# An attention and MLP kernel: eight lead tiles whose scores read the keys in place, and a first block of full-width chunks

## The chip, the core and the metric

The kernel runs on one core of a Trainium2 chip. The metric is device time in microseconds, the median of the timed runs. TensorE (PE) multiplies, VectorE (DVE), ScalarE (ACT) and GpSimd (POOL) work elementwise, SyncE (SP) issues all loads and stores here. A core's engines run side by side, each through its own list in order, and wait for each other by semaphores.

## The reference

Two batches of 768 positions, 8 heads of 64. Each query sees the keys less than 16 positions away and, for every block of 32 keys, one summary key (the maximum over the block) with the mean of its values. The result, 1536 tokens of 512, goes through two layers of MLP (the last two pieces below, 2048 wide inside).

```python
k_sum = k.reshape(B, H, nb, block, D).max(axis=3)
v_sum = v.reshape(B, H, nb, block, D).mean(axis=3)
scores_l = scale * np.matmul(q, k.transpose(0, 1, 3, 2))
...
scores_s = scale * np.einsum('bhsd,bhnd->bhsn', q, k_sum)
scores_s = scores_s + np.log(block)
...
a = np.exp(scores_all)
a = a / (np.sum(a, axis=-1, keepdims=True) + 1e-09)
v_all = np.concatenate([v, v_sum], axis=2)
return np.matmul(a, v_all).astype(np.float32)
...
h = np.maximum(x @ w_in, 0.0)
return (h * h @ w_out).astype(np.float32)
...
h = x @ w_in
g = h * (1.0 / (1.0 + np.exp(-h)))
return (g @ w_out).astype(np.float32)
```

## The kernel before

**Attention** goes by 24 tiles of 64 queries, tiles 0 to 11 for the first batch. A tile's 8 heads are four pairs, two heads on the 128 partitions. `scores` (pss) makes 96 window columns and 24 summary columns at once: two matmuls of 64x120 for each pair. `minima` takes mask and row minimum on VectorE, `exps` the exponentials and their sums z on ScalarE, `inverse` and `norm` scale by 1/z, `transposes` (psa) turns the tile on TensorE, ScalarE copies it (a), `products` (av) multiplies by the values, and `x_high` and `x_low` (xh, xl) split the result into a high and a low half in xt.

**The MLP** goes by three blocks of 512 tokens (eight tiles each) and 16 chunks of the weights. A gemm is 12 matmuls: four parts by three products of high and low halves. gemm1 of chunk s makes h, ScalarE makes relu, square and the high half of g, VectorE the low half (gl), and gemm2 adds to four accumulators (acc). The first layer's weights come as 64-bit floats and are decoded on the fly, chunk by chunk (wi for gemm1, wo for gemm2): ScalarE scales (sc), VectorE shifts, joins sign and low bits (sh, st1, st2), ScalarE writes the high half (hi), VectorE the low one (lo). That is four VectorE steps for each of 32 half chunks, all of them in the first block. Later blocks reuse the split weights.

**The lead.** Tiles 0 to 3 come first. Their key windows are cut by ScalarE (kwl, 16 copies) from the four key tiles of the whole batch, which VectorE also reduces to the 24 maxima (ksum) and copies behind each window (kwsum). Tiles 4 to 7 load their windows and queries as all later tiles do, by two buffers. With four tiles done, the first two chunks begin with 256 columns (TRAIL = 2, HALF = 256); from chunk 2 on 512 columns are taken; and the other 256 columns of chunks 0 and 1 come after chunk 15 as chunks 16 and 17. In the meantime tiles 8 to 15 are worked between the gemms, and the second batch's keys and values are loaded in 16 pieces (kv) and reduced (kvr), each load waiting for the reduction two before it.

**What sets the order.** `first_order` is a list planner: each operation has an engine, a duration, a due time and what it waits for; it takes the operation that can start first and, among those, the one due first. The result is the program order of VectorE, ScalarE, TensorE and SP for the whole first block. From block 1 on a scheduler sets it.

## Time and profile before

| | us |
|---|---|
| median of 3 runs | 626.02 (625.27 to 626.58) |
| profiled execution | 624.39 |
| its span | 622.6 |
| TensorE busy in the span | 603.9 (97%) |
| VectorE busy | 341.4 (55%) |
| ScalarE busy | 302.3 (49%) |

The profile gives each engine's busy time, who released it from a wait, and the clock that TensorE was granted (1.00 is 2.4 GHz, 0.50 is 1.2 GHz). A matmul's start to the next one's start is its price in a row of matmuls; the end in the record holds a tail that overlaps the next. The share of busy time over the whole span says little here, since the first 160 us are another stage than the rest; the tables by stage do. The span leaves out 1.8 us around it.

### The profile page before, as it was taken

How to read it: one execution, taken by the hardware profiler on the slowest of the kernel's cores; microseconds unless marked ns; L12 is line 12 of the kernel's file. 1: busy time of each engine (PE TensorE's matmuls, PEld its weight loads, DVE VectorE, ACT ScalarE, POOL GpSimd, SP SyncE). 2: the span in 40 equal slices, each digit the busy share in tenths (PEclk: the TensorE clock that was granted, in tenths of full speed). 3: DMA queues.
4: the chain of work that ended last, by engine and by line, in shares of the span. 5: the costliest groups of instructions: out<-in, count | busy, mean ns of one | idle time of the engine just before them, and what ended most of it. 6: DMA issues, size and time to landing. Idle time of an engine off the chain costs nothing.

```text
span 622.6 us, 8963 instructions
## 1 busy us (share of the span) xinstructions
PE 603.9 (97%) x3252; PEld 488.1 (78%) x3252; DVE 341.4 (55%) x795; ACT 302.3 (49%) x687; POOL 55.0 (9%) x64
## 2 busy tenths in 40 slices
PE   7789997999999999999999999999999999999997
PEld 5477785777888877888888888888888888888886
DVE  5898998993356444465555686665322222322222
ACT  5876976887535454365454564443222221322221
POOL 0120000000453333100000000000000000000000
PEclk9987999999999999999999999999999999999999
DMA  8987888762455555547653424425400123400301
GB/s 304 313 285 229 263 274 287 229 209 85 141 191 176 185 170 201 172 141 237 200 178 129 136 100 163 178 100 202 152 19 1 67 102 102 135 1 0 102 34 69
DMA packets 37292, 97.51 MB, mean 157 GB/s; under 512 B 4096, under 2 KB 11904, under 8 KB 37248
## 3 DMA queue, kind: packets, MB, share of 16 engines
q1 hardware_dynamic: 37248, 96.93, 47.2%
q8 instruction: 26, 0.43, 0.3%
q14 instruction: 18, 0.15, 0.1%
HBM read 75.94 MB, written 20.97 MB: 156 GB/s over the span
## 4 chain that ended last, share of the span: by engine, by line
PE 78%; DVE 12%; DMA 7%; ACT 1%; SPq 1%; issue 1%; DVEq 0%; ACTq 0%
PE acc L222 37%; PE h L222 37%; DMA t_kv<-in_kT_dram 2%; DMA raw_wi<-in_w_in_dram 2%; PE av L222 2%; DMA raw_wo<-in_w_out_dram 1%; PE pss L222 1%; DMA t_kv<-in_vT_dram 1%; DVE c_wo L282 1%; DVE wi L230 1%; DVE raw_wo L278 1%; DVE raw_wi L278 1%; DVE c_wi L282 1%; DVE wo L230 1%; DVE T L402 1%; DVE g L230 1%
## 5 line engine op out<-in xcount | busy, mean ns | idle before, releaser
L222 PE MATMUL h<-xt,wi 128*128 128x512 f32 (+1 forms) x600 | 146.5, 392 | 3.2 <-DVE wi L230 2.0
L222 PE MATMUL acc<-g,wo 128*128 128x512 f32 (+1 forms) x600 | 141.7, 386 | 0.0
L222 PE MATMUL h<-xt,wj 128*128 128x512 f32 x576 | 139.0, 391 | 0.0
L222 PEld LDWEIGHTS h<-xt,wi 128*128 128x128 f32 x600 | 109.1, 192 | 27.1 <-DVE wi L230 2.8
L222 PEld LDWEIGHTS acc<-g,wo 128*128 128x128 f32 x600 | 110.1, 191 | 22.5 <-issue 0.6
L222 PEld LDWEIGHTS h<-xt,wj 128*128 128x128 f32 x576 | 108.1, 188 | 23.6 <-DVE r L230 0.2
L230 DVE TENSOR_TENSOR g<-r,g 128x512 fp32r<-128x512 f32 (+1 forms) x98 | 80.4, 820 | 79.9 <-ACT g L226 40.7
L230 DVE TENSOR_TENSOR r<-h,r 128x512 f32<-128x512 f32 x48 | 33.2, 691 | 114.2 <-ACT r L529 113.7
L529 ACT ACTIVATE r<-h 128x512 f32<-128x512 f32 x48 | 28.7, 598 | 117.4 <-PE h L222 117.4
L226 ACT ACTIVATE g<-r 128x512 fp32r<-128x512 f32 (+1 forms) x82 | 50.9, 621 | 35.5 <-DVE r L230 34.6
L222 PE MATMUL acc<-wq,g 128*128 128x512 f32 x240 | 57.3, 389 | 0.0
L222 PE MATMUL acc<-wo,g 128*128 128x512 f32 x216 | 53.6, 397 | 0.0
L222 PEld LDWEIGHTS acc<-wq,g 128*128 128x128 f32 x240 | 45.1, 188 | 9.3
L222 PEld LDWEIGHTS acc<-wo,g 128*128 128x128 f32 x216 | 40.7, 188 | 9.7
L411 ACT ACTIVATE T<-T,m 128x120 f32<-128x120 f32 x96 | 36.7, 384 | 20.4 <-DVE m L402 20.3
L222 PE MATMUL acc<-wp,g 128*128 128x512 f32 x120 | 28.8, 389 | 0.0
L227 POOL COPY qd<-qr 128x256 f32<-128x256 f32 x20 | 16.6, 831 | 135.0 <-PE pss L222 97.0
L226 ACT ACTIVATE wo<-c_wo 128x512 fp32r<-128x512 f32 x38 | 23.6, 622 | 7.3 <-DVE c_wo L282 7.2
L521 ACT ACTIVATE r<-h 128x512 f32<-128x512 f32 x16 | 9.6, 598 | 34.7 <-PE h L222 34.7
L222 PEld LDWEIGHTS acc<-wp,g 128*128 128x128 f32 x120 | 22.5, 188 | 4.7
L230 DVE TENSOR_TENSOR wj<-c_wj,wj 128x512 fp32r<-128x512 f32 x16 | 11.1, 692 | 23.7 <-ACT wj L226 23.7
L402 DVE CUSTOM_DVE_ANT_0 T<-pss,cst_sb 128x120 f32<-128x120 f32 x96 | 21.1, 274 | 5.0 <-PE pss L222 4.9
(77 smaller groups left out, 576.9 us busy)
## 6 DMA issues: line engine op xcount, KB each, us to landing
raw_wo<-in_w_out_dram SPq DMA_DIRECT2D x22, 512.0 KB, 4.2
wq<-split SPq DMA_DIRECT2D x20, 512.0 KB, 3.3
raw_wi<-in_w_in_dram SPq DMA_DIRECT2D x16, 512.0 KB, 5.2
split<-wo SPq DMA_DIRECT2D x16, 512.0 KB, 3.4
raw_wj<-in_w_in_dram SPq DMA_DIRECT2D x16, 512.0 KB, 3.7
...
```

The costliest lines, as they stand in the source:

```text
L222: pe.matmul(o, l, r, **kw)
L226: return act.activation(out=o, in_=i, func=AF.Copy, scale=scale)
L227: return eng.tensor_copy(out=o, in_=i)
L230: return eng.tensor_tensor(out=o, in0=a, in1=b, op=op)
L278: vec.scalar_tensor_tensor(out=low, in0=high, scalar=SIGN, in1=low, op0=ALU.bitwise_and, op1=ALU.bitwise_or)
L282: vec.scalar_tensor_tensor(out=c, in0=c, scalar=3, in1=raws.pop(name)[:, :, 0], op0=ALU.logical_shift_left, op1=ALU.bitwise_or)
L402: vec.tensor_tensor_reduce(out=T[:, c], in0=ps[:, c], in1=cst_sb[:, kind * NK:kind * NK + NK], scale=-0.125, scalar=3.0e38, op0=ALU.add, o ...
L411: act.activation(out=T[:, c], in_=T[:, c], func=AF.Exp, bias=m[:, c:c + 1], scale=-1.0, accum_out=z[:, c:c + 1])
L521: act.activation(out=r, in_=h, func=AF.Relu)
L529: act.activation(out=r, in_=h, func=AF.Sigmoid)
```

## The change

NLEAD goes from 4 to 8, and TRAIL and HALF go. Every tile of the first block is now in the lead. Their scores read the keys where they lie: for a tile g and a pair hp the matmul takes 96 columns of the batch's key tile (with 16 zero columns ahead of it) at g x 64, and another one the 24 maxima. So there are no window copies, no copies of maxima behind them and no loads of windows and queries for tiles 4 to 7. The lead's scores (psl), minima (ttl) and exponentials (exl) are planned by pairs instead of whole tiles; queries and values come in two groups of four tiles; the key tiles are loaded with the first queries and the masks between them. The value means are copied to the lead's tiles by two ScalarE copies of 2048 columns (four of 512 before), and to the two buffers of later tiles by ScalarE instead of GpSimd (vfm). Scores and products of the lead use the four accumulator banks. All 16 chunks of the first block take 512 columns. The due times move, and the planner now takes, among the operations of one engine that can start within 0.1 us, the one due first.

```diff
-HALF = 256
-TRAIL = 2
...
-NLEAD = 4
+NLEAD = 8
+NGRP = 4
...
-        return .5 * g if g < NLEAD else 14 + 3 * (g - NLEAD) if g < 2 * NLEAD else 48 + 11 * (g - 2 * NLEAD)
+        return .25 * g if g < NLEAD else 46 + 11 * (g - NLEAD)
...
-    for hp in range(NHP):
-        load("kt", hp, 393, -100 + hp)
-    load("q", 0, 524, -90)
-    load("cst", 0, 250, -89)
-    for c in range(3):
-        load("vr", c, 524, -88 + c)
-    load("vl", 0, 786, -80)
+        return 30 + 7 * s
+
+
+    for i, (name, arg, kb) in enumerate([("kt", 0, 393), ("q", 0, 524), ("kt", 1, 393), ("cst", 0, 250), ("kt", 2, 393),
+                                         ("kt", 3, 393), ("q", 1, 524), ("vr", 0, 524), ("vr", 1, 524), ("vr", 2, 524),
+                                         ("vl", 0, 786), ("vl", 1, 786)]):
+        load(name, arg, kb, -100 + i)
     for hp in range(NHP):
         op("vec", "ksum", hp, 1.0, -50 + hp, [("kt", hp, 0)])
-        op("act", "kwl", hp, .85, -50 + hp, [("kt", hp, 0)])
-    op("vec", "kwsum", 0, .57, -40, [("ksum", hp, 0) for hp in range(NHP)])
...
-        op("pe", "vs", c, .92, 1.2 + .5 * c, [("vr", c // 2, 0)] + [("vs", c - 1, 0)] * (c > 0))
-    op("act", "vmean", 0, 2.2, 3, [("vs", 5, M)])
+        op("pe", "vs", c, .92, 1.7 + .1 * c, [("vr", c // 2, 0)])
+    for i in range(NLEAD // NGRP):
+        op("act", "vmean", i, 1.9, -5, [("vs", c, M) for c in range(6)] + [("vl", i, 0)] * 0)
+    for i in range(NVF):
+        op("act", "vfm", i, .6, tile_due(NLEAD) - 10 + i, [("vmean", 0, 0)])
...
-            op("pe", "pss", g, 1.22, due, [("kwl", hp, A) for hp in range(NHP)] + [("kwsum", 0, A), ("q", 0, 0)])
-            op("vec", "ttr", g, .84, due, [("pss", g, M), ("cst", 0, 0)])
+            for hp in range(NHP):
+                op("pe", "psl", (g, hp), .38, due, [("kt", hp, 0), ("ksum", hp, A), ("q", g // NGRP, 0)] +
+                   [("psl", (g, hp - 1), 0)] * (hp > 0), bank=None if hp else ("acc", "ttl", (g, NHP - 1)))
+                op("vec", "ttl", (g, hp), .21, due, [("psl", (g, hp), M), ("cst", 0, 0)])
+                op("act", "exl", (g, hp), .385, due, [("ttl", (g, hp), A)])
+            exp = [("exl", (g, hp), A) for hp in range(NHP)]
...
-        if g < 2 * NLEAD:
-            op("vec", "nt", g, .78, due, [("zr", g, 0)])
+            op("pe", "pss", g, 1.1, due, [("kwc", g, A), ("side", g, A)] + [("gemm1", 1, 0)] * (g == NLEAD), bank=("att", "ttr", g))
+            op("vec", "ttr", g, .84, due, [("pss", g, M), ("psa", g - 2, M)])
+            op("act", "exp", g, 1.54, due, [("ttr", g, -.45)])
+            exp = [("exp", g, A)]
+        op("vec", "ze", g, .09, due, exp)
+        op("vec", "rc", g, .1, due, [("ze", g, .1)])
+        if g < NLEAD:
...
-    for s in range(NF + TRAIL):
-        due = chunk_due(s) if s < NF else chunk_due(NF - 1) + 6 + 3 * (s - NF)
-        wide = TRAIL <= s < NF
-        p, a, v = (2.72, .57, .61) if wide else (1.44, .34, .36)
-        x = [("xl", g, A) for g in range(NLEAD if s < TRAIL else 2 * NLEAD)]
-        op("pe", "gemm1", s, p, due, x + [("lo", ("wi", s % NF), A)] + [("relu", s - 2, A)] * (s >= 2))
-        op("act", "relu", s, a, due, [("gemm1", s, M)] + [("gl", s - 2, A)] * (s >= 2))
-        op("act", "sq", s, a, due, [("relu", s, 0)])
-        op("act", "gh", s, a, due, [("sq", s, 0)] + [("gemm2", s - 3, M)] * (s >= 3))
-        op("vec", "gl", s, v, due, [("gh", s, A)])
-        op("pe", "gemm2", s, p, due + 5 * LAG, [("gl", s, A), ("lo", ("wo", s % NF), A)] + [("gemm2", s - 1, 0)] * (s > 0))
+    for s in range(NF):
+        due = chunk_due(s)
+        op("pe", "gemm1", s, 2.72, due, [("xl", g, A) for g in range(NLEAD)] + [("lo", ("wi", s), A)] +
+           [("relu", s - 2, A)] * (s >= 2))
+        op("act", "relu", s, .57, due, [("gemm1", s, M)] + [("gl", s - 2, A)] * (s >= 2))
+        op("act", "sq", s, .57, due, [("relu", s, 0)])
+        op("act", "gh", s, .57, due, [("sq", s, 0)] + [("gemm2", s - 3, M)] * (s >= 3))
+        op("vec", "gl", s, .61, due, [("gh", s, A)])
+        op("pe", "gemm2", s, 2.72, due + 5 * LAG, [("gl", s, A), ("lo", ("wo", s), A)] + [("gemm2", s - 1, 0)] * (s > 0))
...
+        t, _, _, o = min((p for p in picks if p[3]["eng"] == o["eng"] and p[0] <= t + .1), key=lambda p: p[1:3])
...
+            T = wo_p.tile([P, NHP, NK], F32, tag="wo", name=f"T{g}") if g < NWO else p2.tile([P, NHP, NK], F32, tag="T", name=f"T{g}")
+            st[g] = dict(v=vlead[:, g], T=T, a=wi_p.tile([P, 512], F32, tag="wi", name=f"a{g}"))
+            small(g)
+        for hp in range(NHP):
+
+            kts[hp] = first_p.tile([P, WIN + S], F32, tag=f"kt{hp}", name=f"t_ksum0_{hp}")
+            pool.memset(kts[hp][:, 0:WIN], 0.0)
...
-        def kwl(hp):
-            for g in range(NLEAD):
-                lo = WIN if g == 0 else 0
-                copy(act, kws[g][:, hp, lo:NWIN], kts[hp][:, g * QT - WIN + lo:g * QT - WIN + NWIN])
-
-        def kwsum(_):
-            for g in range(NLEAD):
-                k_sums(g)
+
+        def psl(ghp):
+            g, hp = ghp
+            if hp == 0:
+                st[g]["ps"] = ps_acc.tile([P, NHP, NK], F32, tag="acc", name=f"pss{g}")
+            q = qrlead[g // NGRP][:, g % NGRP].rearrange("p (q c) -> p c q", c=NHP)
+            for keys, to in ((kts[hp][:, g * QT:g * QT + NWIN], slice(0, NWIN)), (ksum[0][:, hp], slice(NWIN, NK))):
+                for e in range(2):
+                    pr = slice(64 * e, 64 * e + 64)
+                    mm(st[g]["ps"][pr, hp, to], q[pr, hp], keys[pr], start=True, stop=True)
...
-        def vmean(_):
-            for g in range(NLEAD):
-                copy(act, vlead[NWIN:NK, g].rearrange("p h d -> p (h d)"), psv[NWIN:NK])
-            for v in vf:
-                copy(pool, v[NWIN:NK], vlead[NWIN:NK, 0])
+        def vmean(i):
+            means = psv[NWIN:NK]
+            copy(act, vlead[NWIN:NK, i * NGRP:i * NGRP + NGRP].rearrange("p g h d -> p g (h d)"),
+                 bass.AP(means.tensor, means.offset, [means.ap[0], [0, NGRP], means.ap[1]]))
+
+        def vfm(i):
+            copy(act, vf[i][NWIN:NK], vlead[NWIN:NK, 0])
...
-        def cols(s):
-            return slice(HALF if s >= NF else 0, HALF if s < TRAIL else 2 * HALF)
-
         def gemm1_(s):
             h = hs[s] = ps_h.tile([P, 512], F32, tag="h", name=f"h0_{s}")
-            cc = cols(s)
-            gemm1(wi1[s % NF], x, cc.start, cc.stop - cc.start, h[:, cc])
+            gemm1(wi1[s], x, 0, 512, h)
...
-            gemm2(accs, ws["wo", s % NF], gs.pop(s), cc.start, cc.stop - cc.start, s == 0, s == NF + TRAIL - 1, check=False)
+            gemm2(accs, ws["wo", s], gs.pop(s), 0, 512, s == 0, s == NF - 1)
```

On VectorE, at the start: the four key tiles' maxima (ksum), then the copies behind the windows, then minima tile by tile (an ISA row is one minimum of a pair with its accumulator). Before:

```order
L604 TENSOR_REDUCE ksum0_162<-t_ksum0_0_144 128x24
L604 TENSOR_REDUCE ksum0_162<-t_ksum0_1_146 128x24
L604 TENSOR_REDUCE ksum0_162<-t_ksum0_2_148 128x24
L604 TENSOR_REDUCE ksum0_162<-t_ksum0_3_150 128x24
L227 COPY kw0_139<-ksum0_162 128x4x24
L227 COPY kw1_140<-ksum0_162 128x4x24
L227 COPY kw2_141<-ksum0_162 128x4x24
L227 COPY kw3_142<-ksum0_162 128x4x24
L402 ISA T0_226,m0_227<-pss0_208,cst_sb_98 128x120
L402 ISA m0_227 128x1
```

and now:

```order
L615 TENSOR_REDUCE ksum0_201<-t_ksum0_0_180 128x24
L615 TENSOR_REDUCE ksum0_201<-t_ksum0_1_182 128x24
L397 ISA T0_140,m0_142<-pss0_211,cst_sb_98 128x120
L397 ISA m0_142 128x1
L397 ISA T1_145,m1_147<-pss1_218,cst_sb_98 128x120
L397 ISA m1_147 128x1
L397 ISA T2_150,m2_152<-pss2_225,cst_sb_98 128x120
L397 ISA m2_152 128x1
L397 ISA T3_155,m3_157<-pss3_230,cst_sb_98 128x120
L397 ISA m3_157 128x1
L397 ISA T0_140,m0_142<-pss0_211,cst_sb_98 128x120
L397 ISA m0_142 128x1
```

The copies are gone, and the minima of the first pairs stand ahead of the maxima of the last two key tiles.

On TensorE, between the lead's transposes (psa) and the first accumulations: products av of tile g, scores pss, h0_s is gemm1 of chunk s. Before:

```order
L222 MATMUL av0_404<-a0_298,vlead_104 64x64 x8
L222 MATMUL av1_429<-a1_324,vlead_104 64x64 x8
L222 MATMUL av2_449<-a2_342,vlead_104 64x64 x8
L222 MATMUL av3_467<-a3_352,vlead_104 64x64 x8
L432 MATMUL psa4_486<-cst_sb_98,T4_380 120x128 x4
L432 MATMUL psa5_495<-cst_sb_98,T5_415 120x128 x4
L222 MATMUL h0_0_503<-xt0_85,wi0_358 128x256 x12
L222 MATMUL av4_524<-a4_500,vfr0_105 64x64 x8
L222 MATMUL av5_537<-a5_516,vfr1_106 64x64 x8
L222 MATMUL h0_1_554<-xt0_85,wi1_520 128x256 x12
L222 MATMUL pss6_581<-kw6_386,qd0_101 64x120 x8
L222 MATMUL pss7_596<-kw7_413,qd1_102 64x120 x8
```

and now:

```order
L229 MATMUL av0_556<-a0_141,vlead_105 64x64 x8
L229 MATMUL av1_569<-a1_146,vlead_105 64x64 x8
L229 MATMUL av2_580<-a2_151,vlead_105 64x64 x8
L229 MATMUL av3_591<-a3_156,vlead_105 64x64 x8
L229 MATMUL av4_606<-a4_161,vlead_105 64x64 x8
L229 MATMUL av5_619<-a5_166,vlead_105 64x64 x8
L229 MATMUL av6_633<-a6_171,vlead_105 64x64 x8
L229 MATMUL av7_647<-a7_176,vlead_105 64x64 x8
L229 MATMUL pss9_662<-kw9_241,qd1_102 64x120 x8
L229 MATMUL h0_0_681<-xt0_85,wi0_511 128x512 x12
L229 MATMUL h0_1_709<-xt0_85,wi1_656 128x512 x12
L229 MATMUL h0_2_742<-xt0_85,wi2_722 128x512 x12
```

Eight products in a row and one tile's scores now stand ahead of the first gemm, and the first three gemms are of 512 columns.

On TensorE, at the end of the first block (av15 is the last tile's product; acc0_0 to acc0_3 are the accumulators). Before, from chunk 15 on:

```order
L432 MATMUL psa15_1863<-cst_sb_98,T15_1812 120x128 x4
L222 MATMUL h0_16_1868<-xt0_85,wi0_358 128x256 x12
L222 MATMUL av15_1883<-a15_1881,vfr1_106 64x64 x8
L222 MATMUL h0_17_1895<-xt0_85,wi1_520 128x256 x12
L222 MATMUL acc0_0_619<-g0_15_1860,wo15_1762 128x512 x3
```

and now:

```order
L229 MATMUL acc0_3_772<-g0_13_1781,wo13_1677 128x512 x3
L229 MATMUL av15_1859<-a15_1850,vfr1_107 64x64 x8
L229 MATMUL h0_15_1868<-xt0_85,wi15_1824 128x512 x12
L229 MATMUL acc0_0_769<-g0_14_1856,wo14_1740 128x512
L229 MATMUL pss16_2029<-kw16_1956,qd0_101 64x120 x4
L229 MATMUL acc0_0_769<-g0_14_1856,wo14_1740 128x512 x2
L229 MATMUL acc0_1_770<-g0_14_1856,wo14_1740 128x512 x3
```

The half-width h0_16 and h0_17 are gone, and the scores of tile 16, of block 1's attention, stand among the accumulations of chunk 14.

## Rows read from the trace of the kernel before

**Rows 1.** Stages: start:end, length, each engine's busy us (instructions), clock, DMA share, GB/s.

```profile
3.80:48.63 44.83, 36.00 (x352) 26.73 (x350) 37.99 (x158) 34.34 (x119) 5.80 (x8) 0.90 0.94 306
...
61.50:145.70 84.20, 79.39 (x522) 61.44 (x520) 77.57 (x204) 67.95 (x174) 6.60 (x8) 1.00 0.77 244
...
161.00:622.60 461.60, 458.01 (x2218) 374.74 (x2216) 210.89 (x400) 181.00 (x353) 39.27 (x36) 1.00 0.37 125
```

**Rows 2.** Timeline of TensorE: start, us, line, op, out<-in, shape, count; the first block's accumulations.

```profile
48.63 2.93 PE L222 MATMUL acc<-g,wo 128*128 128x256 f32 x12
...
160.03 2.91 PE L222 MATMUL acc<-g,wo 128*128 128x256 f32 x23
```

**Rows 3.** Waits of TensorE, 61.5 to 146 us: who waited for whom, us, times, longest.

```profile
PE h L222 <- DVE wi L230: 2.0, 2, 1.1
PE h L222 <- ACT wi L226: 1.2, 1, 1.2
```

**Rows 4.** Timeline of TensorE, 60 to 69 us.

```profile
60.55 1.04 PE L222 MATMUL pss<-kw,qd 64*64 64x120 f32 x16
61.52 3.03 PE L222 MATMUL h<-xt,wi 128*128 128x512 f32 x12
...
67.12 0.60 PE L432 MATMUL psa<-cst_sb,T 128*120 128x128 f32 x4
67.64 1.04 PE L222 MATMUL pss<-kw,qd 64*64 64x120 f32 x16
```

**Rows 5.** Timeline of TensorE in the lead.

```profile
1.46 6.60 PE L222 MATMUL idle_out<-idle_in 128*128 128x512 f32 x20 [1.46 <-DVE idle_in L576]
10.26 3.14 PE L222 MATMUL pss<-kw,qrlead 64*64 64x120 f32 x48 [2.20 <-DVE kw L227]
13.33 1.04 PE L222 MATMUL psv<-vrows,share 128*24 128x512 f32 x2
...
25.82 0.68 PE L222 MATMUL av<-a,vlead 120*64 120x64 f32 x16
```

**Rows 6.** Weight loads for scores: count, ns min/median/max; strided queries, then packed ones.

```profile
L222 PEld LDWEIGHTS pss<-kw,qrlead x64: 190/213/214, 10.2 to 15.1; 64*64 64x64 f32 x64
...
L222 PEld LDWEIGHTS pss<-kw,qd x16: 130/134/134, 60.6 to 61.2; 64*64 64x64 f32 x16
```

**Rows 7.** Timeline of VectorE: one tile's z to the next minimum, and four minima on.

```profile
13.50 0.17 DVE L417 TENSOR_SCALAR z<-z 128x4 f32<-128x4 f32 x1
...
14.69 0.28 DVE L402 CUSTOM_DVE_ANT_0 T<-pss,cst_sb 128x120 f32<-128x120 f32 x1
...
15.50 0.17 DVE L417 TENSOR_SCALAR z<-z 128x4 f32<-128x4 f32 x1
```

**Rows 8.** Timeline of VectorE: two xl; the first steps of two successive decodes.

```profile
29.04 0.75 DVE L230 TENSOR_TENSOR xt<-av,xt 128x256 fp32r<-128x256 f32 x2
...
50.71 0.42 DVE L274 TENSOR_SCALAR raw_wo<-raw_wo 128x512 int32<-128x512 int32 x1
...
53.11 0.42 DVE L274 TENSOR_SCALAR raw_wi<-raw_wi 128x512 int32<-128x512 int32 x1
```

**Rows 9.** Timelines of VectorE and ScalarE: last maxima, copies of maxima, value means.

```profile
7.74 2.01 DVE L604 TENSOR_REDUCE ksum<-t_ksum 128x24 f32<-128x768 f32 x2 [1.79 <-DMA t_ksum<-in_kT_dram]
9.79 0.57 DVE L227 COPY kw<-ksum 128x96 f32<-128x96 f32 x4
...
22.63 2.04 ACT L226 ACTIVATE vlead<-psv 24x512 f32<-24x512 f32 x4 [0.28 <-PE psv L222]
```

**Rows 10.** Stretches of 2 us, columns as in rows 1.

```profile
28.00:30.00 2.00, 0.66 (x16) 0.52 (x12) 1.97 (x8) 1.98 (x7) 0.00 (x0) 0.78 1.05 396
...
34.00:36.00 2.00, 2.00 (x11) 2.00 (x11) 1.93 (x4) 1.10 (x2) 0.86 (x1) 0.52 0.49 191
36.00:38.00 2.00, 2.00 (x41) 1.80 (x40) 2.00 (x5) 1.73 (x7) 0.00 (x0) 1.00 0.67 223
```

**Rows 11.** Chain that ended last, from 80 us: start, us, what.

```profile
80.39 5.88 DMA t_kv<-in_kT_dram
```

More of the change, by code (lines that the diff above doesn't have):

```diff
@@ L389, in scores, with minimum @@
         st[g]["ps"] = ps
-    def minima(g):
+    def minimum(g, c):
         d = st[g]
@@ L500, in att_steps @@
                 exps(i)
+                guard(i)
                 inverse(i)
@@ L551, in gemm1, with gemm2 @@
             mm(h, w[:, 1, ws], xh, start=False, stop=(k == NKC - 1))
-    def gemm2(acc, w, g, c0, n, first, last, check=True):
+    def gemm2(acc, w, g, c0, n, first, last):
         for k in range(NKC):
@@ L557, in gemm2 @@
             gh, gl = g[:, 0, c0:c0 + n], g[:, 1, c0:c0 + n]
[L558 to L561 removed]
+            mm(o, w[:, 0, ws], gh, start=first, stop=False)
+            mm(o, w[:, 0, ws], gl, start=False, stop=False)
+            mm(o, w[:, 1, ws], gh, start=False, stop=last)
     def finish1(x, acc):
```

151 lines of the change are left out of this document (70 added, 81 removed).

## The prediction

> **What bounds the kernel now.** I read the table by stages first: from 161.0 us to the end TensorE is busy 458.0 of 461.6 us [rows 1], so nothing that the first block does can hide behind the rest, and whatever moves the end of the first block moves the end of the kernel by as much. The change touches only what runs ahead of that point. Second, the first block itself. From 61.5 to 145.7 us TensorE is busy 79.4 of 84.2 us and VectorE 77.6 [rows 1]: two engines are full at once, TensorE a little more so. TensorE's 4.8 us of waits there are mostly for decoded weights [rows 3]. Third, the lead: from 3.8 to 48.63 us TensorE runs 36.0 of 44.8 us, but in it stand only three half-width gemms (a gemm is 12 matmuls, of one weight chunk with the block's columns). The first block's last matmuls, 24 of 256 columns for the two trailing halves, end at 162.9 us with 1.8 us of block 1's work among them [rows 2], so the block's own list ends at about 161.1.
>
> So I keep a ledger: block 1 can start when TensorE has done its list. With A the start of the first full gemm in the changed kernel, the end of the block is A plus the list's work plus waits plus what a low clock costs.
>
> **The list.** One full gemm: in 61.5 to 145.7 us stand 22 gemms, seven tiles' attention and one small transposition group. A tile costs 0.97 us for scores (60.55 to 61.52), 0.52 for transposes (67.12 to 67.64) [rows 4] and 0.61 to 0.68 for the products [rows 5], 2.1 us together. (79.4 - 7 x 2.1 - 0.4) / 22 = 2.92 us. After A the changed kernel has 16 chunks x 2 gemms and tiles 8 to 15: 32 x 2.92 + 8 x 2.1 + 0.4 = 110.6 us. The same sum for the kernel before, from 48.63 us: one half gemm at half clock 2.7, 28 full ones 81.8, four trailing halves 5.9 (2.9 for the two that accumulate [rows 2], 3.0 for the two ahead of them), tiles 17.2, waits 4.8, makes 161.0, which is what the trace has. The trailing halves themselves are worth little: eight halves at 1.5 against four full ones at 2.92 is 0.3 us, and that is in the ledger. With the same 4.8 us of waits the break-even is A + clock cost = 161.1 - 110.6 - 4.8 = 45.7 us.
>
> **Where A comes to stand.** Every tile of the block must now be done first, so A is the end of the lead's chain through TensorE and VectorE.
>
> Scores. ScalarE's 16 copies of the key windows and VectorE's four of the maxima (0.57 us [rows 9]) fall out of the path; in their place each of 32 steps (tile, pair) has four matmuls, two of 96 and two of 24 columns, where there were two of 120. The trace records two entries for each, so eight entries a step. Upper bound: the lead's own score entries, with the same strided queries as weights, follow each other every 3.07 / 48 = 0.064 us [rows 5]; by count that is 0.51 us a step. Lower bound by streamed columns: entries of 64 columns come every 0.68 / 16 = 0.04 us [rows 5], and between 64 and 120 columns 96 gives about 0.051; a 24-column entry as dear as a 64-column one makes 4 x (0.051 + 0.04) = 0.36 us. Which is nearer? Packed queries load in 134 ns, the strided ones in 213 [rows 6], yet the pace only goes from 0.97 / 16 = 0.061 us [rows 4] to 0.064: 79 ns more a load cost 3 ns an entry, so the pace follows columns more than loads. I take 0.40 us.
>
> The Trainium skill, "TensorEngine Tiling (Array Packing)", section Instruction Overhead, says that a matmul of one column takes as long as one of sixty, so that a small dimension should not be split. That rule speaks against cutting 120 columns into 96 and 24. No row here has 24 columns in a score; by the rule a step is the 0.36 us of my lower bound, and A is 0.6 us earlier than below.
>
> TensorE is free of its 20 warm-up matmuls at 8.06 us [rows 5]. Sixteen steps (four tiles by pairs) reach 14.5. Their data are there: in the kernel before the last two key tiles were reduced from 7.74 us on [rows 9]; now 0.77 MB of queries and constants go ahead of the last, 2.5 us at 306 GB/s [rows 1], so its maxima stand at about 12.2, and TensorE comes to that pair at 12.9. VectorE follows one step behind; its first tile is ready to be normalised at 14.4.
>
> From there VectorE's list: z, reciprocal and scaling take 1.19 us a tile (13.50 to 14.69) and a masked minimum 0.2 (four from 14.69 to 15.50) [rows 7]. Six tiles and 17 minima: 7.1 + 3.5 = 10.6, to 25.0. TensorE's other sixteen steps, six groups of transposes and a matmul of the value means end at 14.5 + 6.4 + 3.3 + 0.5 = 24.7, just inside. Then, in VectorE's order up to the last xl: the two last tiles 2.4; whole decodes of wi0 and wo0 4.8, one being the 2.4 us from 50.71 to 53.11 [rows 8]; three of the four decode steps of wi1 and two each of wo1 and wi2, 4.0; eight xl, two of which take 0.75 us and hand over after 0.67 [rows 8], 2.7; two small copies and a reduction 1.1: 15.0, to 40.0. ScalarE's two broadcast copies of the value means (2048 wide; four of 512 took 2.04 us [rows 9], so about 1.9 each) lie beside this, and its two copies for the later value tiles, which GpSimd made, come behind the xh. They hold the first xh until about 33 us, while VectorE comes to its first xl at 35; with that cover gone, each us they come later is one of A. The weights are covered as well: 6.0 MB go ahead of the first raw chunk, at 306 GB/s done by 21.7 us, the chunk by 23.4, wanted at 25. So **A = 40.0 us**, with 39.4 at 0.36 a step. At 0.51 a step the sixteen steps end at 16.2, the first norm begins at 16.1, the last minimum at 28.0, and A is 43.0.
>
> **The clock.** In the kernel before, TensorE was busy 0.66 of 2 us at 28 to 30 us; the granted clock was 0.78 there, still 0.52 at 34 to 36 us though TensorE was full, and 1.00 from 36 on [rows 10]. Half is 1.2 of 2.4 GHz. The changed lead leaves TensorE mostly idle from about 25 to 35 us, so the first gemm probably meets a half clock: it costs 5.4 us in place of 2.9. I charge 2.5 us; bounds 0 (dense products restore it in time) and 5 (two gemms). The Trainium skill, "TensorE: Matmul & The Clock Gate", Part 1, says that idling returns the array to half rate; the rows agree.
>
> **Waits after A.** The decode has less lead than before (three chunks' halves whole and two begun at A, against six at 48.63). By VectorE's order eight more decode steps end wi2 at 40.0 + 4.7 = 44.7; TensorE asks for it behind two gemms, at 48.3. Nine steps and two g later wi3 is there, at 53 at the latest; TensorE asks for it four gemms and a tile's scores in, at 58. So no new wait as long as the first gemm is slow; at full clock some of the 2.5 us saved comes back as waiting. The waits at 95 to 106 us come from the loads of the second batch's keys and values, each of which waits on the reduction two before it, with weight loads behind it on SP's queue; the chain runs through those loads from 80 us on [rows 11]. That pattern is kept, so I keep 4.8 us, with 1.6 and 8 as bounds.
>
> **Sum.** 40.0 + 110.6 + 2.5 + 4.8 = 157.9 us against 161.1: 3.2 us less. The profiled execution took 624.39 us (span 622.6 and 1.8 around it); 621.2 by that. The three timed runs have a median of 626.02, 1.6 us above the profiled one, and the comparison is with them: **622.8 us**. A difference of 0.2%, 1.25 us, is about what can be told from none.
>
> **Rivals.**
> 1. *The score steps are bound by their weight loads* (0.51 us each): A = 43.0, end 160.9, **625.8 us**, no change. For it: the loads double in number, and the strided ones are the only rows with these weights. Against it: the 3 ns above.
> 2. *The waits shrink too*: the first batch of key and value loads starts earlier, the 3.2 us for wi at 95 to 106 us go, and the products restore the clock: 40.0 + 110.6 + 1.0 + 1.6 = 153.2, **618.1 us**. For it: by SP's order the third of these loads goes out near 40 us. Against it: the same queue, the same two buffers for the thirteen left.
> 3. *Slower: the clock falls inside the lead.* Small score matmuls between waits may let it fall as it did at 28 us. Then the last sixteen steps cost twice (6.4 us more) and two gemms run at half (2.5 more than charged): A = 46.4, end 166.8, **631.7 us**. It decides as soon as A and the clock cost together pass 45.7 us, 3.2 above my sum. Against it: the clock was 1.00 through the scores before.
>
> That the change does not do what it says is excluded by the instruction order.
>
> **Chances.** Forecast 0.42, rival 1 0.22, rival 2 0.18, rival 3 (and smaller slips of its kind) 0.18. Faster: 0.42 + 0.18 = 0.60; same 0.22; slower 0.18. The range leaves out half of rivals 2 and 3, under a fifth in all: 618 to 628 us.
>
> **What the profile after would show.** The score entries' spacing in the lead (0.046 to 0.05 us for 0.40 a step, 0.064 for rival 1); the start of the first 512-column gemm at 40 us; a granted clock near 0.5 there for one gemm; waits of TensorE of about 5 us between that and the end of the block; the end of the first block near 158 us and 461.6 us from there to the end. Wrong it would be if the later stage took another time, if ScalarE's value means came after VectorE's xl, or if decoded weights were waited for right behind the first two gemms.

## The result, and the profile after

The changed kernel takes 620.12 us in the median of four runs (619.0 to 621.27), the kernel before 626.03 beside it: a ratio of 0.9907, 95% interval 0.9881 to 0.9932, 5.9 us less. A second comparison, of six runs with seventeen of before, gave 620.10 us and 0.9902 (0.9873 to 0.9932). The prediction was 622.8 us, range 618 to 628, faster the likeliest. The end came out near the forecast, but not by the forecast's own numbers.

The page after: span, then busy time, share and instructions of each engine.

```profile
span 619.2 us, 9053 instructions
PE 606.7 (98%) x3332; PEld 491.2 (79%) x3332; DVE 340.3 (55%) x785; ACT 301.3 (49%) x665; POOL 52.2 (8%) x61
```

Before it was 603.9 us of 622.6. TensorE has 2.8 us more to do, and 12.5 instead of 18.7 us in which it does nothing. The profiled executions differ by 3.4 us of span only. The timed runs of before show granted clocks from 0.981 to 0.995, those of after 0.994 to 1.000, and the profiled one of before, at 0.989, was among its quicker ones.

Stages of after, columns as in rows 1.

```profile
3.80:46.08 42.28, 38.29 (x460) 30.38 (x458) 32.97 (x143) 27.38 (x89) 1.64 (x2) 0.96 0.93 283
...
61.50:161.00 99.50, 96.07 (x601) 74.72 (x600) 81.22 (x210) 78.06 (x195) 8.85 (x9) 1.00 0.70 229
161.00:619.20 458.20, 454.60 (x2192) 371.69 (x2190) 210.28 (x400) 179.64 (x350) 38.66 (x36) 1.00 0.37 125
```

TensorE is idle for 4.0 us in the lead, for 3.4 in the first block and for 3.6 in all that follows; the last figure is that of before [rows 1]. So the gain lies ahead of 161 us, as the prediction had it.

TensorE's timeline of after, columns as in rows 2: end of the warm-up, one score step, the products, the first gemms.

```profile
1.45 7.63 PE L229 MATMUL idle_out<-idle_in 128*128 128x512 f32 x20 [1.45 <-DVE idle_in L581]
...
9.50 0.47 PE L229 MATMUL pss<-t_ksum,qrlead 64*64 64x96 f32 x4
9.80 0.35 PE L229 MATMUL pss<-ksum,qrlead 64*64 64x24 f32 x4
9.98 0.47 PE L229 MATMUL pss<-t_ksum,qrlead 64*64 64x96 f32 x4
...
37.01 2.08 PE L229 MATMUL av<-a,vlead 120*64 120x64 f32 x64 [1.38 <-ACT vlead L233]
41.55 3.63 PE L229 MATMUL av<-a,vlead 120*64 120x64 f32 x64 [2.46 <-DVE xt L237]
...
46.08 8.45 PE L229 MATMUL h<-xt,wi 128*128 128x512 f32 x36
```

A score step takes 0.48 us (9.50 to 9.98), not 0.40. Four products take 2.1 us, the next four, behind a wait of 2.46 us, 3.6. The first gemm starts at 46.08 us, not at 40.0, and then three gemms run at 2.8 us each, at the full clock.

The weight loads of the lead's scores: count, ns min/median/max (compare rows 6).

```profile
L229 PEld LDWEIGHTS pss<-t_ksum,qrlead x128: 188/213/214, 9.0 to 28.4; 64*64 64x64 f32 x128
...
L229 PEld LDWEIGHTS pss<-ksum,qrlead x128: 210/213/214, 9.2 to 28.7; 64*64 64x64 f32 x128
```

The clock, third column from the right, in stretches of 2 us.

```profile
40.00:42.00 2.00, 0.45 (x8) 0.45 (x10) 1.97 (x6) 0.45 (x2) 0.00 (x0) 0.90 0.78 257
42.00:44.00 2.00, 2.00 (x44) 2.00 (x42) 1.59 (x7) 1.28 (x4) 0.00 (x0) 0.50 0.73 270
44.00:46.00 2.00, 2.00 (x40) 1.85 (x36) 1.70 (x6) 1.58 (x4) 0.00 (x0) 0.75 0.33 98
46.00:48.00 2.00, 2.00 (x12) 1.61 (x9) 2.00 (x4) 1.95 (x5) 0.89 (x1) 1.00 0.37 87
```

TensorE's waits from 46 to 161 us (compare rows 3): who waited for whom, us, times, longest.

```profile
PE psa L439 <- ACT T L431: 2.6, 3, 1.4
PE av L229 <- ACT a L233: 0.3, 1, 0.3
PE acc L229 <- DVE g L237: 0.2, 1, 0.2
PE pss L229 <- issue: 0.2, 1, 0.2
```

They make 3.3 us, and none is for decoded weights.

### The profile page after: what moved, and what is told of

Its sections match the earlier page's. It is cut to its first block, busy times and chain, and to the rows that moved or that the text cites. A ratio compares the mean times of both kernels' runs of the same rounds, so it can differ in the third digit from the quotient of the medians.

```text
span 619.2 us, 9053 instructions
## 1 busy us (share of the span) xinstructions
PE 606.7 (98%) x3332; PEld 491.2 (79%) x3332; DVE 340.3 (55%) x785; ACT 301.3 (49%) x665; POOL 52.2 (8%) x61
## 4 chain that ended last, share of the span: by engine, by line
PE 82%; DVE 10%; DMA 4%; ACT 3%; issue 1%; DVEq 0%; ACTq 0%
PE acc L229 37%; PE h L229 37%; PE pss L229 4%; DMA t_kv<-in_kT_dram 2%; PE av L229 2%; PE idle_out L229 1%; DVE c_wo L289 1%; DMA scr_dram<-c_wo 1%; PE psa L439 1%; DVE raw_wi L285 1%; DVE c_wi L289 1%; DVE wi L237 1%; DVE raw_wo L285 1%; DVE wo L237 1%; DMA t_kv<-in_vT_dram 1%
## 5 line engine op out<-in xcount | busy, mean ns | idle before, releaser
L229 PE MATMUL h<-xt,wi 128*128 128x512 f32 x576 | 142.4, 395 | 0.0
L229 PE MATMUL acc<-g,wo 128*128 128x512 f32 x576 | 140.2, 392 | 0.2 <-DVE g L237 0.2
L229 PEld LDWEIGHTS acc<-g,wo 128*128 128x128 f32 x576 | 107.5, 188 | 23.5 <-issue 0.6
L229 PEld LDWEIGHTS h<-xt,wi 128*128 128x128 f32 x576 | 106.5, 188 | 23.0 <-issue 1.0
L237 DVE TENSOR_TENSOR g<-r,g 128x512 fp32r<-128x512 f32 x96 | 80.5, 838 | 74.3 <-ACT g L233 38.4
L233 ACT ACTIVATE g<-r 128x512 fp32r<-128x512 f32 x80 | 50.5, 631 | 35.3 <-DVE r L237 34.5
L234 POOL COPY qd<-qr 128x256 f32<-128x256 f32 x16 | 14.9, 930 | 133.3 <-PE pss L229 85.3
```

The lines of the kernel that those rows point to most:

```text
L229: pe.matmul(o, l, r, **kw)
L233: return act.activation(out=o, in_=i, func=AF.Copy, scale=scale)
L234: return eng.tensor_copy(out=o, in_=i)
L237: return eng.tensor_tensor(out=o, in0=a, in1=b, op=op)
```

## The experiments

Three readings were to be told apart: the gain is less work ahead of the full gemms (the lead); it is the clock that the kernel before loses in the gaps of its lead; it is the order, with fewer waits later. Besides these, what the score step really costs. In the table "first gemm" is the start of the first matmul of 512 columns, and busy, idle and clock are those of the profiled execution; where warm-up matmuls fill waits, they count as busy.

| kernel | median us | ratio to before (95%) | first gemm us | TensorE busy / idle us | clock |
|---|---|---|---|---|---|
| before | 626.0 | 1 | 51.4 | 603.9 / 18.7 | 0.989 |
| after | 620.1 | 0.9907 (0.9881 to 0.9932) | 46.1 | 606.7 / 12.5 | 0.997 |
| after, again | 620.1 | 0.9902 (0.9873 to 0.9932) | 44.6 | 606.1 / 11.8 | 1.000 |
| before, wide chunks alone | 629.0 | 1.0062 (1.0042 to 1.0081) | 46.3 | 605.8 / 21.1 | 0.983 |
| before, waits filled | 624.0 | 0.9966 (0.9946 to 0.9987) | 50.2 | 604.2 / 18.5 | 1.000 |
| after, waits filled | 619.8 | 0.9897 (0.9877 to 0.9916) | 44.4 | 607.6 / 9.1 | 1.000 |
| after, old choice rule | 621.6 | 0.9935 (0.9912 to 0.9958) | 48.0 | 606.6 / 12.5 | 0.994 |
| after, low parts first | 620.4 | 0.9924 (0.9905 to 0.9942) | 41.5 | 605.2 / 13.4 | 0.997 |
| after, windows copied | 617.9 | 0.9876 (0.9854 to 0.9898) | 41.8 | 601.6 / 14.5 | 0.991 |
| the same, waits filled | 616.5 | 0.9841 (0.9815 to 0.9866) | 41.8 | 603.0 / 12.2 | 1.000 |
| after, 12 warm-ups | 618.2 | 0.9883 (0.9866 to 0.9901) | 43.8 | 604.8 / 11.6 | 0.997 |
| after, packed queries | 614.8 | 0.9825 (0.9801 to 0.9849) | 40.6 | 602.7 / 12.1 | 0.993 |
| packed, 12 warm-ups | 614.2 | 0.9816 (0.9794 to 0.9838) | 38.8 | 597.7 / 14.7 | 1.000 |
| the same, one decode later | 613.4 | 0.9804 (0.9774 to 0.9834) | 37.7 | 599.7 / 13.2 | 0.997 |

### One part alone: wide chunks behind the old lead

```diff
-TRAIL = 2
+TRAIL = 0
```

> The kernel before with TRAIL = 0: one part of the change alone. All sixteen chunks of the first block take 512 columns and wait for all eight tiles, while the lead is the old one (four tiles up front, tiles 4 to 7 through their own loads and window copies). Theory L, the gain is the shorter lead: with the old lead the first 512-column gemm can only follow tile 7, whose products ended at 48.7 us in the kernel before; with the two half-width chunks no longer in between (seven gemm halves of 1.7 to 2.9 us out of that stretch) it may come some us earlier or wait all the same, so the start is taken at 46 to 50 us, and the time at 624 to 629 us, no better than before within 0.3% or slower. Theory W, the wide chunks themselves bring it (no gemm of 256 columns, fewer loads of weights, no trailing half pass at 150 to 160 us): at least 4 of the 5.9 us are there, 620 to 622 us, although the old lead stands.

Measured: 0.62% slower than before. The wide chunks do not bring the gain by themselves; behind the old lead they cost 3.9 us. But the start of the first gemm isn't what decides: it comes at 46.3 us, as early as in the changed kernel. TensorE's timeline, two stretches of 2 us and its waits behind the first gemm, to 170 us:

```profile
46.33 0.80 PE L222 MATMUL h<-xt,wi 128*128 128x512 f32 x1 [0.48 <-ACT xt L226]
47.69 7.89 PE L222 MATMUL h<-xt,wi 128*128 128x512 f32 x23 [0.56 <-DVE xt L230]
```

```profile
46.00:48.00 2.00, 1.11 (x2) 0.60 (x3) 2.00 (x5) 1.58 (x3) 0.00 (x0) 0.50 0.82 328
48.00:50.00 2.00, 2.00 (x6) 1.52 (x6) 1.93 (x5) 0.00 (x0) 0.00 (x0) 0.50 0.96 297
```

```profile
PE psa L432 <- ACT T L424: 4.7, 4, 1.7
PE psv L642 <- DVE vsumT L636: 0.8, 1, 0.8
```

Its span is 7.7 us longer than that of after. The second matmul starts 1.4 us later than there; the 23 matmuls from it to the next row, at 55.51 us, take 7.8 us, at the pace of after's first gemms (8.3 us for 36) they would take 5.3, so half the clock costs 2.5; the waits behind are 2.2 longer (5.5 against 3.3); and the scores of a tile, 1.0, which after has done by then, follow. That is 7.1; 0.6 are left over. So 2.5 us of the loss are the clock.

### The clock: waits filled with warm-up matmuls

The kernel before, with matmuls on zeros where TensorE waits in its lead, fifteen by the edit:

```diff
+        for _ in range({6: 3, 7: 2}.get(g, 0)):
+            mm(ps.rearrange("p c q -> p (c q)"), idle[0][:, 0:P], idle[0], start=True, stop=True)
...
+        for _ in range(2 * (g == 7)):
+            mm(av.rearrange("p c q -> p (c q)"), idle[0][:, 0:P], idle[0][:, 0:NHP * QT], start=True, stop=True)
...
+                  pss=filled(scores, {5: 2}), ttr=minima, exp=exps, zr=inverse, nt=lambda g: norm(g, vec if g < 2 * NLEAD else act),
+                  psa=filled(transposes, {4: 1}), a=a_copy, av=filled(products, {1: 2, 2: 3}), xh=xh, xl=x_low, raw=raw, sc=sc,
```

> The kernel before with fourteen short matmuls on zeros where TensorE waits in its lead: two ahead of the scores of tile 5, one, three and two ahead of the transposes of tiles 4, 6 and 7, two, three and two ahead of the products of tiles 1, 2 and 7 (0.2 to 0.33 us each at the full clock, the waits there are 0.5 to 1.3 us). Theory C, a large part of what the change gains is the clock that the kernel before loses in these gaps (granted 0.50 at 30 to 36 us and 0.50 to 0.54 at 46 to 52): the gemm of halves at 33.6 falls from 2.7 to 1.7 us, the one at 48.6 from 2.9 to 1.7, the products and the two gemms behind by 1.4 together, and the time from 625.9 to 622.2 to 624 us, two to three fifths of the change's gain. Rival W: VectorE and ScalarE set when these steps can start, the faster steps turn into longer waits, and the time stays within 0.8 us of before although the clock stays at 1.00. Third: the fillers hold the steps up, 626.5 to 628.

Measured: 0.34% less (0.13 to 0.54), 2.1 us, with the clock at 1.00. The gemms of halves at full clock (compare rows 2), and two lines of its waits from 46 to 165 us:

```profile
32.64 1.68 PE L222 MATMUL h<-xt,wi 128*128 128x256 f32 x12
...
48.63 1.70 PE L222 MATMUL acc<-g,wo 128*128 128x256 f32 x12
```

```profile
PE h L222 <- DVE wi L230: 3.3, 3, 1.8
...
PE h L222 <- ACT wi L226: 1.2, 1, 1.2
```

So the clock is about a third of the gain; by the interval it is anything from a seventh to over a half (0.8 to 3.4 us of 5.9). The waits for decoded weights grow at the same time, from 3.2 to 4.5 us in these lines and by another 1.0 us in the lead (at 36.9 us), so a part of what the clock gave was taken back.

The same for the changed kernel:

```diff
+        def av_(g):
+            for _ in range({0: 3, 4: 6}.get(g, 0)):
+                mm(idle_out, idle_in[:, 0:P], idle_in, start=True, stop=True)
+            products(g)
```

> The changed kernel with nine more of its warm-up matmuls, three ahead of the first product of the lead and six ahead of the fifth, where TensorE waits 1.38 and 2.46 us for ScalarE's means and VectorE's low parts (0.33 us each, so 1.0 and 2.0 us of them lie inside the waits). Theory C, the idle time costs the clock: the granted clock, 0.90, 0.50 and 0.75 between 40 and 46 us now, stays at 1.00, products 4 to 7 take 2.1 us instead of 3.6, the first 512-column gemm starts at 44.4 to 44.8 us and the time is 618.3 to 619 us against 620.1. Rival N: the clock falls all the same, or falls later and on a gemm: no gain, 619.7 to 621 us. Rival D: what stands behind the products (the order of VectorE and ScalarE) does not move, and the 1.5 us come back as waits after 46 us: first gemm earlier, time 619.5 to 620.5.

Measured: 619.8 us. The clock stays up and the products take 2.1 us, as theory C had it, but the ratio does not differ from that of the kernel without. The next run says why. With the waits filled in both kernels their ratios (0.9966 and 0.9897) differ by 0.69%: 4.3 us of the change are left when the clock is held up in both.

> The changed kernel itself once more, beside the next three on the same chip. The first comparison gave 0.9907 (0.9881 to 0.9932) of the kernel before; its profiled run, 621.0 us, was one of its slower ones. Both theories expect 0.990 to 0.992 and 619.5 to 621 us; only a ratio outside 0.988 to 0.993 would change what the other runs are held against.

The same kernel, in this execution:

```profile
41.58 2.08 PE L229 MATMUL av<-a,vlead 120*64 120x64 f32 x64 [2.25 <-DVE xt L237]
```

Nearly the same wait, 2.25 us for 2.46, and the clock did not fall. The half clock of the first profile is no fixed cost of this kernel; it came in one of two profiled executions and was worth 1.5 us there. The ten timed runs fit this: five show granted clocks of 0.994 to 0.997 and took 621.0 us in the mean, five show 0.999 or 1.000 and took 619.1.

### The order: the planner's old choice

```diff
-        t, _, _, o = min((p for p in picks if p[3]["eng"] == o["eng"] and p[0] <= t + .1), key=lambda p: p[1:3])
```

The old 360 for 340 kB per us came back with it.

> The changed kernel with the planner's choice as it was before: strictly the step that can start first, and 360 kB per us for the loads instead of 340. The lead's instructions are the same, their order moves. Theory O, a good part of the 5.9 us is the order that the new rule gives: waits of TensorE after the first 512-column gemm grow from 3.3 to 5 to 8 us (the kernel before had 4.7 there, 3.2 of them for weight parts), time 621.5 to 625 us. Rival L, the lead itself is it: first gemm within 1 us of 46.1, waits within 1.5 us of 3.3, 619 to 621.5 us.

Measured: 0.9935 against 0.9907 and 0.9902, 1.8 to 2.1 us of the gain lost, though the intervals overlap. Neither theory is right as stated: the waits after the first gemm do not grow (2.5 us), the lead does. Its first gemm starts at 48.0 us. In this execution the granted clock was 0.50 from 20 to 26 us, inside the lead, where a tile's transposes took 1.04 us instead of 0.58; its six timed runs show 0.986 to 0.994, all at or below the lowest of after. So what is lost lies in the lead, but how much of it is the order itself and how much the clock is not shown, nor which of the two edits did it.

### Low parts first

```diff
-        op("vec", "sh", (x, s), .35, due, [("raw", (x, s), 0)])
+        op("vec", "sh", (x, s), .35, due, [("raw", (x, s), 0)] + [("xl", 3, 0)] * (2 < i < 6))
```

> The changed kernel with one more dependence in the planner: the decode steps of the fourth to sixth weight chunk on VectorE (each 0.4 to 0.7 us) no longer stand ahead of the low parts of the first four tiles. These low parts free the accumulators that products 4 to 7 need; TensorE waits 2.5 us for them, and its clock falls in that gap, so that products 4 to 7 take 3.6 us instead of 2.1. Theory L: the wait falls from 2.5 to 0.4 to 1.0 us and with it the half clock, products 4 to 7 take 2.1 to 2.9 us, the first 512-column gemm starts at 42.5 to 44 us, and nothing later waits for the postponed decode steps (the chunks concerned are needed 6 us later and more): 616.5 to 618.5 us. Rival theory D: the decode steps that are postponed become late, gemms of the second to fourth chunk wait for their weights, and the gain is given back: 619.5 to 622 us, with waits for low weight parts of 1.5 us and more between 45 and 60 us. Third: only the wait goes and the clock stays low at the same place, 618 to 619 us.

Measured: the first gemm comes 4.6 us earlier, at 41.5 us, and the time is the same, 620.4 us. Rival D is right in kind, though no gemm waits for weights. TensorE's timeline and stretches of 2 us, where ScalarE's scaling comes late:

```profile
80.80 2.93 PE L229 MATMUL acc<-g,wo 128*128 128x512 f32 x12
86.21 1.33 PE L439 MATMUL psa<-cst_sb,T 128*120 128x128 f32 x4 [2.48 <-ACT T L431]
87.19 4.45 PE L229 MATMUL h<-xt,wi 128*128 128x512 f32 x12
91.57 0.69 PE L229 MATMUL av<-a,vfr 120*64 120x64 f32 x16
```

```profile
84.00:86.00 2.00, 0.00 (x0) 0.00 (x0) 1.55 (x6) 0.94 (x3) 0.00 (x0) 1.00 1.07 298
86.00:88.00 2.00, 1.79 (x6) 1.24 (x7) 1.93 (x4) 1.97 (x6) 0.00 (x0) 0.72 0.93 331
88.00:90.00 2.00, 2.00 (x6) 1.52 (x6) 1.96 (x4) 2.00 (x5) 0.00 (x0) 0.50 1.07 360
```

Waits after the first gemm make 6.2 us instead of 3.3. The one of 2.48 us also takes the clock with it: transposes in 0.98 us that take 0.35 elsewhere, a gemm in 4.4 that takes 2.9. 2.9 and 2.1 make 5.0, a little more than the 4.6 gained.

### The score step: packed queries, copied windows

The query windows laid out pair by pair in memory, so that a weight load reads neighbouring columns:

```diff
-            q = qrlead[g // NGRP][:, g % NGRP].rearrange("p (q c) -> p c q", c=NHP)
+            q = qrlead[g // NGRP][:, g % NGRP].rearrange("p (c q) -> p c q", c=NHP)
```

The copy that unpacks later tiles and the array's layout change with it.

> The changed kernel with the query windows laid out pair by pair in memory, so that the score step loads its weights from 64 neighbouring columns instead of every fourth. Nothing else changes. Theory S, strided weight loads set the beat of the score step (213 ns a load in the lead against 130 to 134 ns from the packed tiles, and a beat of 0.120 us for two whether 96 or 24 columns follow): a step falls from 0.48 to 0.29 to 0.41 us, the 32 steps take 9.3 to 13 us instead of 15.4, the loads show 130 to 140 ns; the lead then runs into VectorE, which waits 3.5 us for scores now, so the first 512-column gemm comes 2 to 3.5 us earlier (42.5 to 44 us) and the time is 617 to 618.5 us. Rival theory B, the beat is one of issue and not of loads: the step stays at 0.46 to 0.49 us and the time at 620. Rival theory K, the slow steps are what keeps TensorE busy enough for its full clock up to 40 us: the step falls, TensorE idles between 20 and 35 us, the granted clock falls there and the gemms after it pay, so that under 1 us is left of the gain or nothing (619 to 621 us).

Measured: 614.8 us, 5.1 us less than after by the first ratio and 4.8 by the second, more than theory S asked for. Weight loads, then two score steps:

```profile
L229 PEld LDWEIGHTS pss<-t_ksum,qrlead x128: 129/135/135, 8.4 to 23.2; 64*64 64x64 f32 x128
...
L229 PEld LDWEIGHTS pss<-ksum,qrlead x128: 129/133/133, 8.5 to 23.4; 64*64 64x64 f32 x128
```

```profile
8.66 0.36 PE L229 MATMUL pss<-t_ksum,qrlead 64*64 64x96 f32 x4
8.86 0.25 PE L229 MATMUL pss<-ksum,qrlead 64*64 64x24 f32 x4
8.94 0.36 PE L229 MATMUL pss<-t_ksum,qrlead 64*64 64x96 f32 x4
```

A step is 0.28 us instead of 0.48. Four entries of 96 columns take 0.20 us, four of 24 take 0.08; with strided weights the same took 0.30 and 0.18. VectorE's last minimum in the lead ends at 24.8 us here, at 29.9 in after, and the first gemms run at the full clock:

```profile
40.56 8.50 PE L229 MATMUL h<-xt,wi 128*128 128x512 f32 x36
```

The Trainium skill, "TensorEngine Tiling (Array Packing)", section Instruction Overhead, has a matmul of one column last as long as one of sixty. By that rule 24 columns would cost 60/96, 0.6 of 96 columns, as an estimate from the page's figure. Here they cost 0.4, and the measurement decides.

One part undone: ScalarE copies the windows side by side again, GpSimd the maxima behind them, and a step has half the entries, of 120 columns.

```diff
-            for keys, to in ((kts[hp][:, g * QT:g * QT + NWIN], slice(0, NWIN)), (ksum[0][:, hp], slice(NWIN, NK))):
-                for e in range(2):
-                    pr = slice(64 * e, 64 * e + 64)
-                    mm(st[g]["ps"][pr, hp, to], q[pr, hp], keys[pr], start=True, stop=True)
+            for e in range(2):
+                pr = slice(64 * e, 64 * e + 64)
+                mm(st[g]["ps"][pr, hp], q[pr, hp], klead[g // 2][pr, g % 2, hp], start=True, stop=True)
```

> The changed kernel with one part undone: the scores no longer read the keys where they lie. ScalarE copies each pair's windows side by side (16 copies of two windows, 0.4 to 0.5 us each, 7 us in all, from 3.7 us on, where it is idle until 10.0), GpSimd the sums behind them, and a score step is two matmuls of 120 columns instead of two of 96 and two of 24: 128 weight loads instead of 256 for the lead. Theory R, the loads are the price of reading in place: the step falls from 0.48 to 0.24 to 0.26 us (3.14 us for 48 entries of 120 columns in the kernel before), TensorE's lead gets 7 us shorter, VectorE and the copies become the bound, first 512-column gemm at 42 to 45 us, 616 to 619 us. Theory P, reading in place is what makes the lead of eight tiles short: the copies of the third and fourth pair end at 14 to 16 us, the exponentials stand behind them on ScalarE, the first gemm comes at 46 us or later, 620 to 624 us.

Measured: 617.9 us. Theory R: undoing the part that reads keys in place makes the kernel faster, by 1.9 us against the first ratio of after and 1.6 against the second, although the clock falls on its first gemms. The intervals overlap, so by these numbers alone it is at least not slower. TensorE's timeline of these gemms:

```profile
42.92 10.88 PE L231 MATMUL h<-xt,wi 128*128 128x512 f32 x35 [0.34 <-DVE xt L239]
53.63 5.60 PE L231 MATMUL acc<-g,wo 128*128 128x512 f32 x24
```

The same kernel with warm-up matmuls in TensorE's waits, fifteen by the edit:

```diff
+                  pss=filled(scores, {9: 2}), ttr=minima, exp=exps, ze=guard, rc=inverse, psl=psl, ttl=lambda a: minimum(*a),
...
+                  psa=filled(transposes, {7: 2}), a=a_copy, av=filled(products, {0: 2, 4: 4, 7: 3}), xh=xh, xl=x_low, raw=raw, sc=sc,
...
+                  st2=lambda xs: dec_join(name(xs), cs[xs]), scr=scr_, hi=hi, lo=lo, gemm1=filled(gemm1_, {0: 2}), relu=relu, sq=sq, gh=gh,
```

> The kernel with copied windows (617.9 us; clock granted at 0.50 from 42 to 48 us, its first three gemms 10.9 us where the changed kernel needs 8.5) with thirteen warm-up matmuls in the waits of TensorE between 29 and 42 us. Theory C: the clock stays at 1.00, the first 512-column gemm stays at 41.8 to 43 us, the three gemms take 8.4 to 8.8 us, time 615.2 to 616.2 us: then copying beats reading in place with strided weights by 3.5 to 4.5 us at the same clock. Rival: the fillers stand in front of the steps and the first gemm moves back by 1 to 2 us, so that little or nothing is gained: 616.8 to 618.5 us.

```profile
42.87 8.23 PE L231 MATMUL h<-xt,wi 128*128 128x512 f32 x35 [0.62 <-DVE xt L239]
50.93 5.60 PE L231 MATMUL acc<-g,wo 128*128 128x512 f32 x24
```

Measured: 616.5 us, 2.2 less by the ratios, with the first gemm where it was. The 35 matmuls take 8.1 us instead of 10.7: the clock's price when it falls on gemms is 2.6 us. This ratio's interval lies wholly below both of after's.

### A shorter warm-up, and the best of these together

```diff
-WARM = 20
+WARM = 12
```

> The changed kernel with 12 instead of 20 warm-up matmuls, so that TensorE is free at about 6.1 instead of 9.0 us. Theory L, the beginning of the scores counts: the steps of the first pair of heads, whose keys and maxima are there at 4.7 us, start about 2.9 us earlier; the steps of the second pair must wait for keys that arrive at 8.1 us and their maxima at 9.0, so four to six steps of 0.48 us, 2 to 2.9 us, come off the lead unless VectorE's order of work (maxima of pair 1 ahead of the steps) holds them back; first 512-column gemm at 43.2 to 45 us, time 617.2 to 619 us. Rival: VectorE and the later keys are the bound of the lead, not TensorE's start, and the first gemm moves by under 0.7 us: 619.5 to 621 us. Third: the clock, no longer at its upper level when the scores begin, makes the steps slower and eats the gain (619.5 to 623 us, granted clock near 0.5 in 6 to 15 us).

Measured: scores start at 6.5 instead of 9.0 us, the first gemm at 43.8, and 618.2 us, 1.5 us less by the first ratio, 1.2 by the second, with intervals that overlap those of after. With packed queries:

> The two edits that gained apart, together: packed query windows (614.8 us, first 512-column gemm at 40.6) and 12 warm-up matmuls (618.2 us against 620.1 without, first gemm 2.3 us earlier). Theory: with packed weights TensorE is no longer the bound of the lead, so that its earlier start is worth less than alone; keys of pairs 1 to 3 land at 8 to 12 us and VectorE, busy from 9.7 us on, sets the pace: first gemm at 39.0 to 40.5 us, 613.2 to 614.8 us. Rival, both are additive: first gemm at 38.3 us, 612.5 to 613 us. Third: fewer columns before 9 us and idle time of TensorE behind, the granted clock falls inside the lead and on the first gemms: 614.8 to 617 us.

Measured: 614.2 us. The first gemm moves by 1.8 us, the time by 0.6, inside the intervals; TensorE now waits for VectorE's minima. And with one decode chunk put behind the low parts:

```diff
-        op("vec", "sh", (x, s), .35, due, [("raw", (x, s), 0)])
+        op("vec", "sh", (x, s), .35, due, [("raw", (x, s), 0)] + [("xl", 3, 0)] * (i == 4))
```

> Packed query windows and 12 warm-up matmuls (614.2 us) with one decode chunk (the third of w_in) put behind the low parts of the first four tiles on VectorE, which is a third of what the run with all low parts first moved. TensorE's wait for the low parts is 2.0 us there. Theory: two decode steps of 0.42 and 0.69 us leave the queue ahead of the first low part, the wait falls to 0.9 to 1.2 us, the first gemm comes 0.8 to 1.1 us earlier (37.7 to 38 us instead of 38.8), the rest keeps its order: 613.1 to 613.6 us. Rival: as when all were moved, ScalarE's order shifts and tile waits of 2 us and more appear between 60 and 160 us: 614 to 616 us.

Measured: 613.4 us, 0.9804 of before; the wait for low parts is 1.0 us instead of 2.0. It is the best version here, 2.0% under the kernel before and 1% under the changed one, though the last two edits are not told apart from none by their intervals.

## Why the prediction was right or wrong, step by step

**The ledger** held. TensorE's timeline of after at the end of the block:

```profile
153.02 0.63 PE L229 MATMUL pss<-kw,qd 64*64 64x120 f32 x8
...
156.20 3.33 PE L229 MATMUL h<-xt,wi 128*128 128x512 f32 x14
...
159.60 0.84 PE L229 MATMUL h<-xt,wi 128*128 128x512 f32 x3
160.28 2.66 PE L229 MATMUL acc<-g,wo 128*128 128x512 f32 x11
```

Block 1's 17 matmuls (4.1 us at the list's price of a gemm, 3.9 by their starts) and eight score entries of tile 16 (0.5) stand ahead of the last accumulations, which end at 162.9 us, so the block's own list ends at 158.3. The start of 46.1, a list of 109.6 (110.6 less the scores of tile 9, which are done by then) and 3.3 us of waits make 159.0. The 0.7 are 0.02 us a gemm. The forecast was 157.9. From 158.3 us to the end of the span it takes 460.9 us, 0.6 less than from 161.1 in the kernel before; what those 0.6 are no run here shows.

**The start of the first gemm** failed: 46.1 us (44.6 in the second profile) for 40.0. The mis-sized term is the score step, 0.48 us for 0.40, almost rival 1's 0.51. The argument was that 79 ns more a load cost 3 ns an entry [rows 4 to 6], so columns set the pace. What failed is the division behind it: a row's time over its entries also spreads what the two ends of the row cost, and the rows compared hold 16 entries and 48. The trace of before has a second row of each kind, at the same clock of 1.00, and the difference of two rows leaves the ends out:

```profile
14.30 1.22 PE L222 MATMUL pss<-kw,qrlead 64*64 64x120 f32 x16
15.45 0.65 PE L432 MATMUL psa<-cst_sb,T 128*120 128x128 f32 x4
...
38.92 1.86 PE L222 MATMUL pss<-kw,qd 64*64 64x120 f32 x32
40.71 1.69 PE L222 MATMUL acc<-g,wo 128*128 128x256 f32 x12
```

Packed queries: 32 entries take 1.79 us, 16 take 0.97 [rows 4], so an entry is 0.051 us. Strided ones: 48 take 3.07 [rows 5], 16 take 1.15, so an entry is 0.060. The columns are 120 in all four rows, so the strided loads already set the pace there, by 9 ns an entry and not 3. Eight entries at 0.060 make 0.48 us, which is what a step of 96 and 24 columns took in after. The packed run is the proof: the same columns, and a step of 0.28. VectorE's last minimum in the lead, 25.0 us in the forecast:

```profile
29.64 0.28 DVE L397 CUSTOM_DVE_ANT_0 T<-pss,cst_sb 128x120 f32<-128x120 f32 x1
```

It ends at 29.9. Of the delay of 4.9 us, 0.95 is the warm-up, 7.63 us instead of 6.60, and 2.6 is the step, 32 times 0.08; the other 1.4 were not broken down. From there to the gemm it took 16.2 us, not 15.0, with one tile's scores (1.0) and the slow products (1.5) in it.

**The clock** was charged 2.5 us, and nothing was paid on gemms. TensorE had work to 35.6 us, where the forecast had it mostly idle from 25 on, and the half clock met products only, in one execution of two. That the one is the reason for the other is not shown: the packed kernel's lead is shorter by 5 us, and its first 36 matmuls of 512 columns take 8.5 us, as in after. With copied windows the first gemms did meet the half clock, and paid 2.6 us, as forecast.

**The waits** were 3.3 us for 4.8. Those for decoded weights are gone. They are also absent with the old choice rule and in the run of wide chunks alone, so they go with the two chunks taken by halves (TRAIL = 2) and the planned times that hang on them; which of these makes them wait was not isolated.

**The sum** came out because these cancel: 6.1 us later, 2.5 without the clock, 1.5 fewer waits, 1.0 of the list done earlier, and 0.7 in the gemms leave +0.4 at the block's end. That is luck: no run gives a reason why the late start and the unpaid clock and waits should be of one size. Rival 1 had the mechanism and still missed the time, since it kept the other terms. Rival 2 was right that waits and clock would cost less, without its early start. Against the profiled execution the forecast was 621.2, and 621.0 was measured. The 2.7 us between 622.8 and 620.1 lie between profiled execution and median: that of before is 1.6 us under its median, that of after 0.9 over.

**Where the gain is.** The clock is 2.1 us of 5.9 (0.8 to 3.4 by the interval), by filling the gaps of the kernel before. The rest can't be given to one part: the wide chunks lose 3.9 us without the new lead, and the new lead without the new rule loses about 2. Reading the keys in place, as it was made, takes nothing off: with copies the kernel is 1.6 to 1.9 us faster by the ratios, and 3.5 when both have their waits filled (0.9841 and 0.9897, intervals apart). With packed queries, reading in place is as good as copies with strided queries and filled waits, or better (0.9825 and 0.9841, overlapping intervals). Copies with packed queries were not run, so which of the two ways is better once the queries are packed stays open.
